# Spreading the decays of a chunked scan from three bfloat16 parts, with the early order of the program anew

## The chip, the cores and the metric

One core of one Trainium2 chip. The metric is the device time of one execution in microseconds (us); before, it is 664.39 us, the median of 3 runs (663.97 to 665.87).

## The reference

A chunked linear-attention scan, then a gated (GLU) layer, then a squared-ReLU layer:

```
la = log(clip(a, 1e-6, 1)); cum = cumsum(la)             # 4 batches, 8 heads, 768 steps
y[i] = sum_{j<=i} (C_i . B_j) exp(cum_i - cum_j) x_j  +  carried state, decayed
g, v = y @ w_gate, y @ w_val                             # 3072 x 256 @ 256 x 1536
z = (silu(g) * v) @ w_out                                # 1536 -> 256
out = relu(z @ w2_in)**2 @ w2_out                        # 256 -> 2048 -> 256
```

The inputs come as 32-bit floats, the weights as 64-bit floats, which the kernel converts. It splits operands into a high and a low fp32r part and sums three products (high x high, high x low, low x high), or runs some parts "exact" as plain fp32, which TensorE does in two passes.

## The kernel before

**The work.** The scan goes over 28 chunks of at most 112 steps (seven per batch). For a chunk, the decays `a` of its eight heads are spread over all 128 partitions, a scan on VectorE turns them into the decay matrix `L`, TensorE makes the scores `cb`, VectorE multiplies both into `mt`, and eight products `ys` give the outputs; the state goes through `st`, `turn` and back into `xa` for the next chunk. The GLU layer then runs in cells (a weight pair `j`, a range of chunks, exact or not): products `g` and `v`, a tanh on ScalarE, two multiplications on VectorE (`gate`, `times`), a split of the result on ScalarE and GpSimd (not for exact cells), and products into `acc`. The last layer runs over six tiles of 512 tokens.

**The early stage.** The first seven chunks (batch 0, `k < EARLY`) are handled differently from the 21 later ones. Their decays are spread by TensorE: `spread` (L548) multiplies a column of `pick`, broadcast, with the decays in `dv_all`, four heads to one PSUM tile `ab`, 56 fp32 products in all. Later chunks read the spread decays from DRAM (`decay`), where `keep_decays` (L333) stores them. `zeros` (L234) clears unused rows of `dv_all`, `load_a` (L244) loads, and `clip` (L252) bounds the values. Meanwhile the weight units are converted from 64-bit words: `share` and `mag` on ScalarE, `sign`, `clamp` and `shift` on VectorE (L380 to L406), then split into `hi` on ScalarE (`top`) and `lo` on GpSimd (`rest`, L412).

**The order.** Nothing is scheduled by the hardware: `Graph.order` (L50) simulates engines with a table of costs (the second argument of `g.add`), picks on each engine the ready operation with the lowest `prio`, and the program issues its instructions in that order. Each engine then runs its queue strictly in order, SP's queue of loads included. `PLAN` (L1027) holds priorities of chunks, weight units, splits and cells. Where the order leaves TensorE a gap of at least 110 ns before an operation that opens a PSUM tile, in the first 70 us of its own clock, `new` (L209) fills it with idle products of 256 columns:

```
if op.start - free >= 110:
    fills.append(int((op.start - free) / 110))
```

**The end.** `relu2` (L853) drains the last tile's two sums from PSUM in four half copies of 256 columns, two by ScalarE and two by VectorE, each with a store of its own (L909 to L933).

Of the kernel before, what the change touches and what calls it, by code (L numbers as in the profile page):

```python
# [8 lines left out]
F32 = mybir.dt.float32  # L9
# [25 lines left out]
class Graph:  # L35
# [14 lines left out]
    def order(self):  # L50
# [12 lines left out]
        while left:  # L63
            started = True
            while started:
                started = False
                for eng, ops in avail.items():
# [3 lines left out]
                    need = {}  # L71
                    for op in ops:
                        if best is not None and op.prio > best.prio:
                            continue
# [6 lines left out]
                        if all(len(free[p]) >= k for p, k in need.items()):  # L81
                            best = op
# [45 lines left out]
def kernel(  # L128
# [74 lines left out]
    dv = dv_all[0:R]  # L203
# [29 lines left out]

    def zeros():  # L234
# [4 lines left out]
        r = R  # L239
        while r < P:  # L240
            nc.vector.memset(dv_all[r : 2 * r], 0.0)
            r *= 2

    def load_a():  # L244
        v = a.rearrange("b h s -> (b h) s")
        nc.sync.dma_start(
            out=dv[:, :full, 1:], in_=v[:, : full * Q].rearrange("p (c q) -> p c q", c=full)
        )
        if full < NCB:
            nc.sync.dma_start(out=dv[:, full, 1 : 1 + S - full * Q], in_=v[:, full * Q :])  # L250

    def clip():  # L252

        for v in (dv[:, :full, 1:], dv[:, full:, 1 : 1 + S - full * Q]):
            nc.vector.tensor_scalar(v, v, 1e-6, 1.0, op0=ALU.max, op1=ALU.min)
# [39 lines left out]
    def setup_pick():  # L295
        nc.gpsimd.memset(pick, 0.0)
        nc.gpsimd.affine_select(
            out=pick, in_=pick, pattern=[[-1, H]], base=0,
            channel_multiplier=1, compare_op=ALU.not_equal, fill=1.0,
        )  # L300
# [14 lines left out]
    op_pick = g.add("POOL", 280, setup_pick, prio=-999)  # L315
# [12 lines left out]

    op_zero = g.add("DVE", 1000, zeros, prio=-960)
    ld_a = dma("SP", 2, 450, 200, load_a, [], -950)  # L330
    op_clip = g.add("DVE", 900, clip, [ld_a, op_zero], -950)

    def keep_decays(b):  # L333
        nc.sync.dma_start(
            out=decay[b].rearrange("c h q -> h c q"), in_=dv[b * H : (b + 1) * H]
# [3 lines left out]
        b: dma("SP", 1, 450, 400, lambda b=b: keep_decays(b), [op_clip], 300 + b)  # L339
# [84 lines left out]
    def chunk_ops(k, prio, after=(), load_after=()):  # L424
# [27 lines left out]
        if early:  # L452
# [9 lines left out]
            lb = dma("SP", 1, 480, 650, lambda: load_b(0, B), [op_eb[k % NEB], *load_after], ldp, [e])  # L462
            lc = dma("SP", 1, 480, 650, lambda: load_b(1, C), [op_eb[k % NEB], *load_after], ldp, [e])
# [622 lines left out]
```

## Time and profile before

| | before |
|---|---|
| median of 3 runs | 664.39 us |
| the profiled execution, its span | 664.27 us, 662.5 us |
| TensorE busy | 654.8 us, 99% of the span |
| VectorE, ScalarE, GpSimd busy | 63%, 50%, 34% |
| VectorE busy in the first 70 us | 58.1 us |
| TensorE's granted clock | 1.00 in every slice |

Times count from the start of the span. A row of the timeline gives start, length and the count of merged instructions; products are pipelined, their ends are modelled, and the end of one lies past the start of the next, so a rate is read from start to start. An idle product is named by the tile that it writes (`ab<-idle`).

### The profile page before, as it was taken

How to read it: one execution, taken by the hardware profiler on the slowest of the kernel's cores; microseconds unless marked ns; L12 is line 12 of the kernel's file. 1: busy time of each engine (PE TensorE's matmuls, PEld its weight loads, DVE VectorE, ACT ScalarE, POOL GpSimd, SP SyncE). 2: the span in 40 equal slices, each digit the busy share in tenths (PEclk: the TensorE clock that was granted, in tenths of full speed). 3: DMA queues.
4: the chain of work that ended last, by engine and by line, in shares of the span. 5: the costliest groups of instructions: out<-in, count | busy, mean ns of one | idle time of the engine just before them, and what ended most of it. 6: DMA issues, size and time to landing. Idle time of an engine off the chain costs nothing.

```text
span 662.5 us, 10931 instructions
## 1 busy us (share of the span) xinstructions
PE 654.8 (99%) x4297; PEld 560.9 (85%) x4297; DVE 415.5 (63%) x578; ACT 329.3 (50%) x634; POOL 221.9 (34%) x207
## 2 busy tenths in 40 slices
PE   9999999999999999999999999999999999999997
PEld 7888677899877777777788889999999999999996
DVE  7898796667565756677455698454455544544553
ACT  4667444455544444555544584444444444444443
POOL 4005864947555656656564541000000000000000
PEclk9999999999999999999999999999999999999999
DMA  7767447476465456752422220000000100000000
GB/s 176 210 129 153 134 84 145 88 134 123 100 126 94 81 108 113 171 129 50 142 64 63 64 65 0 1 33 1 1 33 0 33 1 1 33 1 0 33 1 33
DMA packets 134819, 48.88 MB, mean 74 GB/s; under 512 B 120304, under 2 KB 123376, under 8 KB 134768
## 3 DMA queue, kind: packets, MB, share of 16 engines
q1 hardware_dynamic: 134480, 47.92, 32.7%
q8 instruction: 34, 0.56, 0.4%
q10 hardware_dynamic: 288, 0.26, 0.1%
q14 instruction: 17, 0.14, 0.1%
HBM read 33.94 MB, written 3.22 MB: 56 GB/s over the span
## 4 chain that ended last, share of the span: by engine, by line
PE 97%; DMA 1%; SPq 0%; ACT 0%; issue 0%; DVE 0%; ACTq 0%
PE acc L892 21%; PE h L701 20%; PE g L701 18%; PE acc L819 16%; PE v L701 13%; PE ys L648 2%; PE ab L552 1%; PE cb L619 1%; DMA raw<-in_moe_w_val_dram 1%; PE ab L225 1%; PE cb L610 1%; PE turn L687 1%; PE g L225 1%; PE cb L225 0%; PE trb L225 0%
## 5 line engine op out<-in xcount | busy, mean ns | idle before, releaser
L892 PE MATMUL acc<-hi,p 128*128 128x256 f32 x768 | 152.1, 282 | 0.0
L892 PEld LDWEIGHTS acc<-hi,p 128*128 128x128 f32 x768 | 125.5, 191 | 3.9
L792 POOL TENSOR_TENSOR p<-t,p 128x512 fp32r<-128x512 f32 (+4 forms) x74 | 98.0, 1326 | 91.4 <-ACT p L787 89.3
L873 DVE TENSOR_TENSOR t<-t 128x512 f32<-128x512 f32 x96 | 69.2, 722 | 66.1 <-ACT t L870 66.0
L892 PE MATMUL acc<-lo,p 128*128 128x256 f32 x384 | 108.6, 283 | 0.0
L880 DVE TENSOR_TENSOR p<-t,p 128x512 fp32r<-128x512 f32 x96 | 67.8, 709 | 57.2 <-ACT p L876 57.2
L870 ACT ACTIVATE t<-h 128x512 f32<-128x512 f32 x96 | 57.5, 599 | 78.6 <-PE h L701 78.3
L768 DVE SCALAR_TENSOR_TENSOR t<-t,g 128x512 f32<-128x512 f32 (+6 forms) x92 | 51.9, 565 | 71.1 <-ACT t L765 71.0
L876 ACT ACTIVATE p<-t 128x512 fp32r<-128x512 f32 x96 | 60.5, 632 | 63.4 <-DVE t L873 59.9
L819 PE MATMUL acc<-p,hi 128*128 128x512 f32 (+4 forms) x296 | 85.7, 372 | 0.0
L892 PEld LDWEIGHTS acc<-lo,p 128*128 128x128 f32 x384 | 73.3, 191 | 3.5
L701 PE MATMUL h<-xh_all,hi 128*128 128x512 f32 x192 | 75.8, 395 | 0.0
L701 PE MATMUL h<-xl_all,hi 128*128 128x512 f32 x192 | 75.8, 395 | 0.0
L701 PE MATMUL h<-xh_all,lo 128*128 128x512 f32 x192 | 74.7, 389 | 0.0
L787 ACT ACTIVATE p<-t 128x512 fp32r<-128x512 f32 (+4 forms) x74 | 42.2, 571 | 62.5 <-DVE t L771 58.9
L765 ACT ACTIVATE t<-g 128x512 f32<-128x512 f32 (+6 forms) x92 | 46.1, 503 | 45.3 <-PE g L701 42.6
L701 PE MATMUL g<-xh_all,hi 128*128 128x512 f32 (+4 forms) x176 | 64.4, 366 | 0.0
L701 PE MATMUL g<-xh_all,lo 128*128 128x512 f32 (+4 forms) x176 | 61.4, 349 | 0.0
L701 PE MATMUL g<-xl_all,hi 128*128 128x512 f32 (+4 forms) x176 | 61.3, 349 | 0.0
L819 PEld LDWEIGHTS acc<-p,hi 128*128 128x128 f32 x296 | 52.1, 188 | 10.3 <-issue 2.9
L771 DVE SCALAR_TENSOR_TENSOR t<-t,v 128x512 f32<-128x512 f32 (+2 forms) x66 | 42.9, 649 | 21.6 <-PE v L701 17.2
L415 POOL TENSOR_TENSOR lo<-v,hi 128x1024 fp32r<-128x1024 f32 x17 | 42.8, 2535 | 32.2 <-ACT hi L410 32.0
(97 smaller groups left out, 1148.6 us busy)
## 6 DMA issues: line engine op xcount, KB each, us to landing
ab<-decay SPq DMA_DIRECT2D x21, 452.0 KB, 4.3
raw<-in_moe_w_out_dram SPq DMA_DIRECT2D x14, 512.0 KB, 5.1
raw<-in_moe_w_in_dram SPq DMA_DIRECT2D x8, 512.0 KB, 4.0
raw<-in_moe_w_gate_dram SPq DMA_DIRECT2D x6, 512.0 KB, 4.0
raw<-in_moe_w_val_dram SPq DMA_DIRECT2D x6, 512.0 KB, 5.1
xa<-in_x_dram SPq DMA_DIRECT2D x24, 112.0 KB, 4.1
out_dram<-o SPq DMA_DIRECT2D x10, 256.0 KB, 2.2
bc<-in_B_dram SPq DMA_DIRECT2D x18, 56.0 KB, 2.5
```

Of the source, the lines that this page charges most:

```text
L415: e.tensor_tensor(self.lo.t, self.v.t, self.hi.t.bitcast(F32), op=ALU.subtract)
L701: nc.tensor.matmul(ps, l, r, start=(i == 0), stop=(i == len(terms) - 1))
L765: nc.scalar.activation(t[:, :n], gg(), AF.Tanh, scale=0.5)
L768: nc.vector.scalar_tensor_tensor(tb.t[:, :n], tb.t[:, :n], 1.0, gg(), op0=ALU.add, op1=ALU.mult)
L771: nc.vector.scalar_tensor_tensor(tb.t[:, :n], tb.t[:, :n], 0.5, vv(), op0=ALU.mult, op1=ALU.mult)
L792: e.tensor_tensor(p[:, 1, :n], tb.t[:, :n], p[:, 0, :n].bitcast(F32), op=ALU.subtract)
L819: nc.tensor.matmul(ps, l, r, start=bank not in done_f, stop=f == NF - 1, skip_group_check=True,)
L870: nc.scalar.activation(new(tb, [P, TN], F32, "t"), ph.t, AF.Relu)
L873: nc.vector.tensor_tensor(tb.t, tb.t, tb.t, op=ALU.mult)
L876: nc.scalar.activation(new(pb, [P, 2, TN], F32R, "p")[:, 0, :], tb.t, AF.Copy)
L880: e.tensor_tensor(pb.t[:, 1, :], tb.t, pb.t[:, 0, :].bitcast(F32), op=ALU.subtract)
L892: nc.tensor.matmul(ps, pb.t[:, l, tk], r, start=(f == 0 and s == 0 and q % 2 == 0), stop=(f == NF2 - 1 and s == 2), skip_group_check=True,)
```

## The change

1. `dv` holds the decays three times (rows 0 to 31, 32 to 63, 64 to 95), and four steps, `part1`, `rest1`, `part2`, `rest2`, on ScalarE and VectorE in turn, make three bfloat16 parts of them in `dp`, whose sum is the fp32 value to about 24 bits. `spread` runs once over 96 rows in bfloat16, with ones of `pick` at each part's row. It is done in three lots: the first chunk, the next five, the last. The copies of later batches are stored from rows 64 to 95, which stay whole.
2. `Graph.order` puts an operation on VectorE or GpSimd that would need the port the other holds back, if that one will last more than 200 ns (`dodge`).
3. The low parts of two weight units are made on VectorE instead of GpSimd (`lo` in `PLAN`).
4. The last tile's sums leave in two copies of 512 columns, the first by VectorE, the second by ScalarE, with one store each.
5. Some costs of the table are set anew (the B, C and x transfers, the spread), and so are the priorities in `PLAN`.

```
+                    other = busy.get({"DVE": "POOL", "POOL": "DVE"}.get(eng))
                     for op in ops:
-                        if best is not None and op.prio > best.prio:
+                        at = op.prio
+                        if op.port and other and other.port and other.start + other.took > now + 200:
+                            at = (at[0] + PLAN["dodge"], at[1])
+                        if best is not None and at > best_at:
                             continue
...
-    pick = const.tile([P, H], F32, name="pick")
+    pick = const.tile([3 * R, H], BF16, name="pick")
-    dv_all = const.tile([P, NCB, Q + 1], F32, name="dv")
+    dp = const.tile([3 * R, NCB, Q + 1], BF16, name="dp")
...
+    dv_buf = Buf("ab")
+    dv = new(dv_buf, [P, NCB, Q + 1], F32, "dv")[0 : 3 * R]
...
+    def part1(c0, c1):
+        nc.scalar.activation(dp[:, c0:c1], dv[:, c0:c1], AF.Copy)
+    def rest1(c0, c1):
+        r = slice(0, 2 * R)
+        nc.vector.tensor_tensor(dv[r, c0:c1], dv[r, c0:c1], dp[r, c0:c1], op=ALU.subtract)
+    def part2(c0, c1):
+        nc.scalar.activation(dp[0 : 2 * R, c0:c1], dv[0 : 2 * R, c0:c1], AF.Copy)
+    def rest2(c0, c1):
+        r = slice(0, R)
+        nc.vector.tensor_tensor(dp[r, c0:c1], dv[r, c0:c1], dp[r, c0:c1], op=ALU.subtract)
...
+    for (c0, c1), at in zip(((0, 1), (1, full), (full, NCB)), PLAN["decay_at"]):
...
-        b: dma("SP", 1, 450, 400, lambda b=b: keep_decays(b), [op_clip], 300 + b)
+        b: dma("SP", 1, 450, 400, lambda b=b: keep_decays(b), op_clip, 300 + b, [dv_buf])
...
-                            v[:, j, :], pick[:, h : h + 1].to_broadcast([P, P]), dv_all[:, k, :],
+                            v[:, j, :], pick[:, h : h + 1].to_broadcast([3 * R, P]), dp[:, k, :],
...
-                o = g.add("PE", 1000, spread, [op_clip, op_pick, before.scans[-1] if before else None], prio, [ps, c.L], lat=250)
+                o = g.add("PE", 310, spread, [parts[k], op_pick, before.scans[-1] if before else None], prio, [ps, c.L], lat=250)
...
-            cuts = 2 if i == T // TN - 1 else 1
+            end = i == T // TN - 1
+            cuts = 1
...
-                    by_act = (m if cuts == 1 else c) == 0
+                    by_act = m == (1 if end else 0)
...
-        W1[u].split(abs(at) * 100, "POOL", [last_unit] if at < 0 else [])
+        W1[u].split(abs(at) * 100, "DVE" if PLAN["lo"][units.index(u)] else "POOL", [last_unit] if at < 0 else [])
...
-    chunk_at=[3.6, 14.8, 21.8, 0.0, 3.2, 18.0, 18.5],
+    chunk_at=[0, 18.4, 25.5, 1.0, 9.6, 12.8, 10.3],
...
+    dodge=3000,
+    lo=[0, 0, 0, 0, 0, 1, 1, 0, 0],
```

Over the whole program the order has 56 spread products before and after; idle products go from 119 to 179; fp32 products of 112 columns in the cells go from 48 to 24, fp32r products of 208 columns from 36 to 0, and those of 432 columns from 108 to 144.

VectorE's queue at the start, before: setup, the clips of `dv`, then scans of `ab` into `L` between the passes of the first weight units (`raw`, `v`).

```order
L241 MEMSET dv 32x791
L241 MEMSET dv 64x791
L255 TENSOR_SCALAR dv<-dv 32x6x112
L255 TENSOR_SCALAR dv<-dv 32x96
L561 SCALAR_TENSOR_TENSOR L<-ab,delta 128x452 x2
L395 SCALAR_TENSOR_TENSOR raw<-raw 128x1024
L400 TENSOR_SCALAR v<-v 128x1024
L404 SCALAR_TENSOR_TENSOR v<-v,raw 128x1024
L561 SCALAR_TENSOR_TENSOR L<-ab,delta 128x452 x2
L634 TENSOR_TENSOR mt_107<-cb,L 128x4x112 x2
```

The same place in the changed program (`dp` holds the parts; L599 is the scan, L672 the multiplication by the scores, L433 to L442 the weight unit):

```order
L264 TENSOR_SCALAR dv<-dv 96x112
L273 TENSOR_TENSOR dv<-dv,dp 64x113
L280 TENSOR_TENSOR dp<-dv,dp 32x113
L599 SCALAR_TENSOR_TENSOR L<-ab,delta 128x452 x2
L264 TENSOR_SCALAR dv<-dv 96x5x112
L672 TENSOR_TENSOR mt_107<-cb,L 128x4x112 x2
L433 SCALAR_TENSOR_TENSOR raw<-raw 128x1024
L438 TENSOR_SCALAR v<-v 128x1024
L709 TENSOR_TENSOR xl_all<-ys,xh_all 128x2x112
L442 SCALAR_TENSOR_TENSOR v<-v,raw 128x1024
L273 TENSOR_TENSOR dv<-dv,dp 64x565
```

The long memsets are gone, the first lot's subtractions stand before the first scan, and the second lot's clip and subtractions stand between the passes of the first weight unit, where the scan of the second chunk stood.

SP's queue of loads at the start, before (`eb` takes B and C of a chunk, `xa` its x, `raw` a weight unit):

```order
L246 DMA dv<-in_a_dram 32x6x112
L250 DMA dv<-in_a_dram 32x96
L374 DMA raw<-in_moe_w_out_dram 128x2x512 x2
L457 DMA eb_100<-in_B_dram 112x8x16
L457 DMA eb_100<-in_C_dram 112x8x16
L446 DMA xa_104<-in_x_dram 112x8x32
L374 DMA raw<-in_moe_w_gate_dram 128x2x512
L374 DMA raw<-in_moe_w_val_dram 128x2x512
L334 DMA decay<-dv 8x7x113 x3
```

and after:

```order
L253 DMA dv<-in_a_dram 96x1x112
L484 DMA xa_104<-in_x_dram 112x8x32
L495 DMA eb_100<-in_B_dram 112x8x16
L495 DMA eb_100<-in_C_dram 112x8x16
L412 DMA raw<-in_moe_w_gate_dram 128x2x512
L412 DMA raw<-in_moe_w_val_dram 128x2x512
L256 DMA dv<-in_a_dram 32x5x112 x3
L412 DMA raw<-in_moe_w_out_dram 128x2x512 x2
L253 DMA dv<-in_a_dram 96x1x96
```

The first chunk's x, B and C now stand ahead of all weights, a gate and value unit is loaded first, the loads of the second and third lot come behind it, and the stores of `decay` have moved further back, behind the loads of chunks 1 to 3.

TensorE's queue at the second chunk, before (L552 is the spread, L610 the scores):

```order
L468 MATMUL trb<-eye,eb_101 128x128 x2
L552 MATMUL ab<-dv,pick 128x113 x4
L648 MATMUL ys<-mt_107,xa_104 32x128 x8
L552 MATMUL ab<-dv,pick 128x113 x4
L610 MATMUL cb<-bct 128x112 x8
L687 MATMUL turn<-eye,st 16x128 x2
```

The same place in the changed program (L506 is the transposition, L739 the products `g` of an exact cell, L229 the filler):

```order
L506 MATMUL trb<-eye,eb_101 128x128 x2
L229 LDWEIGHTS idle
L229 MATMUL g<-idle 128x256
L739 MATMUL g<-xf,v 128x112 x8
L229 LDWEIGHTS idle
L229 MATMUL ab<-idle 128x256
...
L590 LDWEIGHTS pick
L590 MATMUL ab<-dp,pick 128x113
...
L648 MATMUL cb<-bct 128x112 x8
```

The output of the first chunk and its turn now stand ahead of this place, exact products of 112 columns have come in between, filler is spread around it, and each bfloat16 product has its weight load as an instruction of its own.

## Rows read from the trace of the kernel before

**Rows 1.** The chain that ended last, share of the span by engine.

```profile
PE 97%; DMA 1%; SPq 0%; ACT 0%; issue 0%; DVE 0%; ACTq 0%
```

**Rows 2.** TensorE's waits after the start: for what, us in total, times, longest.

```profile
PE turn L687 <- ACT st L682: 1.3, 1, 1.3
...
PE ys L648 <- issue: 1.1, 1, 1.1
```

**Rows 3.** Timeline of TensorE, first 75 us: start, us, line, operation, shape, count.

```profile
1.14 5.90 PE L225 MATMUL ab<-idle 128*128 128x256 bf16 x32 [1.14 <-DVE idle L207]
6.87 1.94 PE L552 MATMUL ab<-dv,pick 128*128 128x113 f32 x16
8.65 1.58 PE L225 MATMUL ab<-idle 128*128 128x256 bf16 x13
...
14.23 1.15 PE L610 MATMUL cb<-bct 64*128 64x112 f32 x16
...
17.93 0.64 PE L648 MATMUL ys<-mt,xa 128*32 128x128 f32 x16
...
28.89 0.94 PE L701 MATMUL g<-xf,v 128*128 128x224 f32 x4
...
64.46 0.65 PE L648 MATMUL ys<-mt,xa 112*32 112x128 f32 x16
```

**Rows 4.** The spread's group over the whole span: busy us, mean ns, idle before.

```profile
L552 PE MATMUL ab<-dv,pick 128*128 128x113 f32 x112 | 14.2, 276 | 0.0
```

**Rows 5.** Timeline of TensorE near 88 us, with bfloat16 scores of a late chunk.

```profile
88.12 0.57 PE L619 MATMUL cb<-bct 128*128 128x112 bf16 x8
88.50 0.44 PE L701 MATMUL v<-xh_all,hi 128*128 128x432 f32 x1
88.79 0.36 PE L701 MATMUL v<-xl_all,hi 128*128 128x432 f32 x1
88.98 0.36 PE L701 MATMUL v<-xh_all,lo 128*128 128x432 f32 x1
```

**Rows 6.** Timeline of TensorE near 105 us, products of 208 columns.

```profile
104.99 0.27 PE L701 MATMUL g<-xl_all,hi 128*128 128x208 f32 x1
105.10 0.27 PE L701 MATMUL g<-xh_all,lo 128*128 128x208 f32 x1
```

**Rows 7.** Timeline of VectorE, 13 to 64 us.

```profile
13.23 2.08 DVE L561 TENSOR_TENSOR_SCAN L<-ab,delta 128x452 f32<-128x452 f32 x2
15.41 1.16 DVE L634 TENSOR_TENSOR mt<-cb,L 128x448 f32<-128x448 f32 x2
16.48 1.22 DVE L395 SCALAR_TENSOR_TENSOR raw<-raw 128x1024 uint32<-128x1024 uint32 x1
17.61 0.68 DVE L400 TENSOR_SCALAR v<-v 128x1024 f32<-128x1024 f32 x1
18.33 1.22 DVE L404 SCALAR_TENSOR_TENSOR v<-v,raw 128x1024 uint32<-128x1024 uint32 x1
19.47 0.38 DVE L671 TENSOR_TENSOR xl_all<-ys,xh_all 128x224 fp32r<-128x224 f32 x1
...
34.11 0.39 DVE L771 SCALAR_TENSOR_TENSOR t<-t,g 128x224 f32<-128x224 f32 x1
...
60.40 3.31 DVE L404 SCALAR_TENSOR_TENSOR v<-v,raw 128x1024 uint32<-128x1024 uint32 x1
```

**Rows 8.** DMA issues by line: count, KB each, median us from issue to landing.

```profile
out_dram<-o SPq DMA_DIRECT2D x10, 256.0 KB, 2.2
...
out_dram<-o SPq DMA_DIRECT2D x2, 128.0 KB, 1.7
```

**Rows 9.** Timeline of ScalarE near 23 us, a weight conversion and what released it.

```profile
22.98 1.10 ACT L389 ACTIVATE raw<-raw 128x1024 int32<-128x1024 uint16 x1 [3.65 <-DMA raw<-in_moe_w_val_dram]
```

**Rows 10.** Line of the late scores: weight loads and products, ns min/median/max.

```profile
L619 PEld LDWEIGHTS <-bct x168: 95/98/102, 88.1 to 320.1; 128*128 128x128 bf16 x168
L619 PE MATMUL cb<-bct x168: 206/213/226, 88.1 to 320.1; 128*128 128x112 bf16 x144, 128*128 128x96 bf16 x24
```

More of the change, by code (lines that the diff above doesn't have):

```diff
@@ L237, in zeros, with load_a, clip @@
             nc.vector.memset(dv[:, full, 1 + S - full * Q :], 0.0)
[L239 to L244, printed above, removed]
-        v = a.rearrange("b h s -> (b h) s")
[L246 to L255, printed above, removed]
+    def load_a(c0, c1):
+        v = a.rearrange("b h s -> (b h) s")
+        t0, n = c0 * Q, min(Q, S - c0 * Q)
+        if c1 - c0 == 1:
+            src = v[:, t0 : t0 + n]
+            src = bass.AP(src.tensor, src.offset, [[0, 3], [S, R], [1, n]])
+            nc.sync.dma_start(out=dv[:, c0, 1 : 1 + n], in_=src)
+        else:
+            for i in range(3):
+                nc.sync.dma_start(
+                    out=dv[i * R : (i + 1) * R, c0:c1, 1 : 1 + n],
+                    in_=v[:, t0 : t0 + (c1 - c0) * n].rearrange("p (c q) -> p c q", c=c1 - c0),
+                )
+    def clip(c0, c1):
+        v = dv[:, c0:c1, 1 : 1 + min(Q, S - c0 * Q)]
+        nc.vector.tensor_scalar(v, v, 1e-6, 1.0, op0=ALU.max, op1=ALU.min)
+    def part1(c0, c1):
[8 more added lines that the diff above has]
+        nc.vector.tensor_tensor(dp[r, c0:c1], dv[r, c0:c1], dp[r, c0:c1], op=ALU.subtract)
     def setup_dve():
@@ L296, in setup_pick @@
         nc.gpsimd.memset(pick, 0.0)
[L297 to L300, printed above, removed]
+        for i in range(3):
+            nc.gpsimd.affine_select(
+                out=pick, in_=pick, pattern=[[-1, H]], base=-i * R,
+                channel_multiplier=1, compare_op=ALU.not_equal, fill=1.0,
+            )
     def setup_bc():
@@ L925, in store @@
                     def store(ob=ob, by_act=by_act, r0=t0 + m * 256 + c * (w // 2)):
-                        q = nc.scalar if by_act and cuts == 2 else nc.sync
+                        q = nc.scalar if by_act and end else nc.sync
                         q.dma_start(
@@ L932, in relu2 @@
                     o = g.add("ACT" if by_act else "DVE", 690 // cuts, drain, [bk], prio - GATE, [ab[m], ob])
-                    dma("ACT" if by_act and cuts == 2 else "SP", 1, 480, 700, store, [o], prio, [ob])
+                    dma("ACT" if by_act and end else "SP", 1, 480, 700, store, [o], prio, [ob])
         return o1, bk
@@ L1027 @@
 PLAN = dict(
-    chunk_at=[3.6, 14.8, 21.8, 0.0, 3.2, 18.0, 18.5],
-    unit_at=[4.1, 0, 22.6, 19.4, 20.4, 41.5, 34.2, 27.1, 30.0],
-    split_at=[-0.1, -21.6, 22.5, -12.5, -9.6, 27.7, -0.1, -18.9, -33.9],
+    chunk_at=[0, 18.4, 25.5, 1.0, 9.6, 12.8, 10.3],
+    unit_at=[0.6, 14.2, 26.4, 24.5, 25.5, 36.5, 42.9, 26.0, 29.8],
+    split_at=[-1.7, -37.7, 65.8, -3.7, 4.5, -30.7, -27.2, 49.0, 13.5],
     cells=[
+        (2, 3, 7, 0),
+        (4, 0, 3, 0),
+        (3, 3, 7, 0),
         (5, 3, 7, 0),
-        (4, 0, 3, 0),
+        (1, 3, 7, 1),
+        (3, 0, 3, 0),
+        (4, 3, 7, 0),
+        (0, 3, 7, 1),
+        (1, 0, 3, 0),
+        (0, 1, 3, 1),
         (5, 0, 3, 1),
-        (3, 3, 7, 1),
         (2, 0, 2, 1),
-        (0, 3, 7, 1),
-        (4, 3, 7, 0),
-        (0, 1, 2, 1),
-        (2, 5, 7, 0),
-        (1, 3, 7, 0),
-        (2, 2, 3, 1),
-        (0, 0, 1, 1),
-        (0, 2, 3, 1),
-        (3, 0, 3, 0),
-        (1, 0, 3, 0),
-        (2, 3, 5, 1),
-    ],
-    pace=[-5, 2.65, 13],
-    second=[34, 5, 6],
+        (0, 0, 1, 1),
+        (2, 2, 3, 1),
+    ],
+    pace=[-5, 2.67, 9],
+    second=[20, 6, 1],
     gate=[30000, 30000],
     lead=2.5,
+    decay_at=[-950, 381, 1562],
     spare=0,
     warm=70000,
+    dodge=3000,
+    lo=[0, 0, 0, 0, 0, 1, 1, 0, 0],
 )
```

30 lines of the change are left out of this document (20 added, 10 removed).

## The prediction

> **What bounds the kernel.** I read the chain of waits first: 97% of the chain that ends last is TensorE's own work [rows 1]. TensorE's list of waits then has only two after the start, 1.1 us before an output `ys` and 1.3 us before a `turn`, 2.4 us in all [rows 2]. TensorE is thus never short of work, but in the first 68 us part of that work is filler: 119 idle products, which the order puts where its table expects TensorE to wait [rows 3]. So two things set the time: how long TensorE's real products take, and how much filler and waiting the first stage still needs. What VectorE, ScalarE or GpSimd save later costs or gains nothing, unless it makes TensorE wait.
>
> All sums are made against the profiled execution, 664.27 us, which is 0.12 us under the median of the runs (664.39). What lies around the span stays as it is.
>
> **1. The spread.** Before, 56 fp32 products spread the decays, and each shows as two passes: 112 passes, a group of 14.2 us [rows 4]. The rows of the timeline run a little past the start of what follows; from start to start the first 16 passes take 8.65 - 6.87 = 1.78 us [rows 3], 0.111 each, which makes 12.5 us for seven chunks. Between 12.5 and 14.2 I take 13.0. After, there are 56 bfloat16 products of 113 columns over 96 rows. The nearest row is the bfloat16 scores, eight of 112 columns in 88.50 - 88.12 = 0.38 us, 0.0475 each [rows 5]; so 2.7 us. If one bfloat16 product took as long as one fp32 pass (0.111) it would be 6.2. I take the nearer row: **minus 10.3 us** (minus 6.8 at the other end). Each new product has a weight load of its own, and so have those eight.
>
> The Trainium skill, in "TensorE: Matmul & The Clock Gate", section "Back-to-back issue gap", puts a stream of weight load and product pairs with 128 columns at some 81 ns a pair. By it the spread would be 4.5 us and the sum 1.8 us higher, an estimate. The eight scores of this trace ran at 47.5 ns, so the row decides.
>
> **2. The order of cells anew.** Counted over both programs, 24 fp32 products of 112 columns go (48 passes at 0.111: 5.3 us), 36 products of 208 columns go (105.10 - 104.99 = 0.11 each: 4.0 us [rows 6]), and 36 of 432 columns come (88.98 - 88.79 = 0.19 to 0.2 each [rows 5]: 7.0 us). **Minus 2.3 us**. It falls due on TensorE, so all of it counts.
>
> **3. The filler.** 119 idle products become 179. Thirteen have a row of 1.58 us, less the 0.16 it runs over: 1.42, 0.109 each [rows 3]. The first 32 took 5.7 us, 0.18 each, and I take that for the first 32 of after too. Sixty more at 0.109: **plus 6.5 us**. They cannot be skipped once they stand in the queue: this part of the gain is given back for certain.
>
> **4. Waits beyond the filler.** The two of before (2.4 us) go with their places; what comes is the open cost. Without any wait the sum is 664.27 - 10.3 - 2.3 + 6.5 - 2.4 = 655.8 us, the floor. For the new waits I follow the two busiest engines to the output `ys` of the last early chunk.
> - TensorE: 1.1 us to begin, 173 fillers (5.7 + 141 x 0.109 = 21.1), the spread 2.7, seven scores at 1.08, six earlier outputs at 0.57, eleven fp32 sets of 224 columns at 0.77, 24 passes of 112 columns at 0.111 [rows 3] (each row less the 0.07 to 0.17 by which it runs past the next start), and 13 pairs of turns at two such passes, 2.9: together 49.8 us.
> - VectorE: its first scan needs 42 fillers, a transposition and four spreads, so it starts near 8.7 us. From there to the last scores' multiplication stand 14 scans at 1.04, 14 multiplications at 0.535, five weight units at 1.13 + 0.72 + 1.14, five `xl_all` at 0.38 less 0.08, five pairs of gate products (three at 2 x 0.39, two shorter) 3.4 [rows 7], and of the decays two clips and four subtractions. For the latter the nearest row is again the `xl_all` subtraction, 0.38 us for 224 elements, and the weight unit's pass, 1.2 us for 1024: between them 565 elements cost about 0.75 and 113 about 0.28, with the clips 2.7 us. Together 44.7, so 53.4 us if VectorE never idles.
>
> VectorE arrives 3.6 us after TensorE. So TensorE waits **plus 3.6 us** in this stage; afterwards its products of 432 columns last longer than what VectorE does for them, and it sets the pace again. The ends: nothing, if VectorE's passes overlap better than start to start; 5 us, if it idles a little between.
>
> **5. What I cost at nothing.** The six ScalarE copies (about 2.5 us by the same lengths) and the first lot's five steps lie under the first 42 fillers, which end near 8.0 us; without that cover the first scan would be later by what they exceed. The port rule moves work, it adds none: it can spare VectorE a collision like the 3.31 us that one 1.2 us pass took while GpSimd made low parts [rows 7], and that one came where TensorE did not wait. The memsets that go (two long ones of the unused rows) lay before VectorE's first scan, where it waits anyway. On SP's queue the x load of the first chunk now passes B and C, and both weight loads of the unit stand behind them: no weight transfer is ahead of B and C any more, so the transposition is not later than its filler. The decay stores now wait for the third clip, and behind them stand weight and B/C loads of chunk 3, covered by 31 fillers (3.4 us) around its transposition. Two low parts move from GpSimd to VectorE late, behind products of 336 columns; TensorE has other cells in its queue there, and the list of waits had none there [rows 2]. At the end two half copies on each engine become one of 512: the last copy starts sooner, since nothing precedes it on its bank, but a store of 256 KB lands in 2.2 us, of 128 KB in 1.7 [rows 8]. I take zero, with 0.5 either way.
>
> **Sum:** 655.8 + 3.6 = **659.4 us**, minus 0.7%.
>
> **The rivals.**
> - **Loads come late.** The two waits of before both began on ScalarE, which stood behind a weight load: 3.65 us in the first [rows 9], while outputs and turns were queued behind it. The changed order still has weight conversions ahead of turns on ScalarE. One such wait that VectorE cannot absorb adds 3.65: 663.0 us; half of it, 661.2. For: SP issues more small loads ahead of the first weights. Against: the filler is longer, so there is more cover. Chance 0.17, a third of it still under 662.3.
> - **The filler covers everything.** If VectorE's stage packs as the table of costs assumes, the waits vanish: 655.8 us. Against it stands the sum of VectorE's rows. Chance 0.08.
> - **The weight loads set the pace of the spread.** One of bfloat16 takes 98 ns [rows 10]; if 56 of them do not overlap they make 5.5 us, 2.8 more than taken: 662.2. Against: the same loads stood before the eight quick scores. Chance 0.06.
> - **Slower: the second lot of decays stops VectorE.** Its clip, two copies and two subtractions stand in the queues of VectorE and ScalarE among the first weight units, and its load is issued behind a unit's 1 MB. Both queues keep their order, so a late load stops all early chunks at once. Three waits of the size in rows 9 make 11 us: 670.4. It decides from 6.9 us of idle VectorE (659.4 to 666.3), after which the change is slower. For: it is a new five-step chain between two full engines. Against: the spread that needs the second lot stands some ten microseconds after the first. Chance 0.07.
>
> That a bfloat16 product would still run as two passes I leave without a chance: the late scores are 21 chunks of eight products, and the trace has 168 of them, one pass each [rows 10].
>
> **How the numbers follow.** My forecast has 0.62: 657.8 to 660.8 for waits of 2 to 5 us. A measurement of this kernel tells about 0.3%, 2 us, from no change, so faster means under 662.4. Faster: 0.62 + 0.08 + 0.06 + a third of the late loads, 0.06, makes 0.82. Same: the rest of them, 0.11. Slower: 0.07. The range goes from the floor, 655.8, to 663.0, the late-load case; only the slower case and what lies past one late load stay outside.
>
> **What would show it.** In the profile after: the spread's group at 56 products and about 3 us from start to start; 179 idle products; TensorE's list of waits with 2 to 5 us in the first 60 us, most of it released by VectorE's multiplications `mt` or by what follows from them; the last early output near 53 to 55 us, where it was at 64.5 [rows 3]; no wait later. Wrong would be: waits over 6 us, a wait behind a load, or any in the stage of 512 columns.

## The result, and the profile after

The changed kernel takes **671.25 us** (median of 4 runs, 670.61 to 672.26) against 664.18 (663.55 to 665.87) for the kernel before on the same chip: ratio 1.0113, 95% interval 1.0098 to 1.0127. It is slower by 1.1%, where 0.7% faster was forecast. The profiled execution took 671.73 us, with a span of 669.8.

On the page, the chain that ended last, by engine, which answers to [rows 1]:

```profile
PE 83%; DMA 6%; DVE 5%; ACT 2%; issue 1%; SPq 1%; POOL 1%; DVEq 0%; POOLq 0%; ACTq 0%
```

TensorE made 97% of it before. TensorE's waits (for what, us in total, times, longest us), which answer to [rows 2]:

```profile
PE acc L857 <- DVE t L809: 2.2, 2, 1.2
PE g L739 <- ACT xf L701: 1.7, 1, 1.7
PE trb L229 <- DVE dv L242: 1.1, 1, 1.1
PE ys L686 <- POOL mt L632: 1.1, 1, 1.1
PE g L739 <- DVE lo L453: 1.0, 1, 1.0
PE trb L506 <- DMA eb<-in_B_dram: 0.7, 1, 0.7
```

TensorE's timeline, which answers to [rows 3]:

```profile
7.24 0.38 PE L506 MATMUL trb<-eye,eb 128*128 128x128 f32 x2
7.46 0.56 PE L590 MATMUL ab<-dp,pick 96*128 96x113 bf16 x8
7.86 1.58 PE L229 MATMUL cb<-idle 128*128 128x256 bf16 x13
...
55.22 0.64 PE L686 MATMUL ys<-mt,xa 112*32 112x128 f32 x16
...
60.22 1.72 PE L739 MATMUL g<-xf,v 128*128 128x432 f32 x4 [1.74 <-ACT xf L701]
```

The eight new spread products run from 7.46 to 7.86, 0.05 us each from start to start, and the last early output stands at 55.2 where it was at 64.46 [rows 3]. So the last early output comes 9.2 us sooner, and the program takes 7 us longer. The page's group of the spread, which answers to [rows 4], has 56 products; each overlaps the next, so its busy time is above 56 x 0.05 = 2.8:

```profile
L590 PE MATMUL ab<-dp,pick 96*128 96x113 bf16 x56 | 4.1, 213 | 0.0
```

The wait of 1.74 us at 60.22 is explained on ScalarE. Its timeline there, which answers to [rows 9]:

```profile
58.61 1.10 ACT L427 ACTIVATE raw<-raw 128x1024 int32<-128x1024 uint16 x1 [3.67 <-DMA raw<-in_moe_w_val_dram]
59.61 0.34 ACT L803 ACTIVATE t<-g 128x224 f32<-128x224 f32 x1
59.85 0.32 ACT L701 ACTIVATE xf<-ys 128x192 f32<-128x192 f32 x1
```

ScalarE stood 3.67 us before a weight conversion, because the load had not landed; the copy `xf` of the last early output was queued behind it, and TensorE waited for `xf`.

To see where the time went I use four starts on TensorE's timeline, in us: the last early output, the first product of 512 columns, the first `h` of the last layer, and the last product. They are read from the profiled execution of each kernel that the text needs; `e1` to `e17` and `b1` are the experiments of the next section. The execution of e7 was 1.9 us above the median of its runs, those of the others in the table within 0.8:

| kernel | early output | first 512 | first `h` | last product |
|---|---|---|---|---|
| before | 64.5 | 169.1 | 385.1 | 658.2 |
| changed | 55.2 | 171.2 | 390.9 | 665.5 |
| e1: changed, 32 bytes of padding | 55.9 | 170.7 | 387.0 | 660.2 |
| e7: e1, spread four times | 62.0 | 174.2 | 390.5 | 663.8 |
| e10: e1, longer conversions | 55.6 | 176.8 | 393.1 | 666.4 |
| e12: e1, shorter conversions | 56.5 | 168.3 | 384.7 | 657.9 |
| b1: before, bfloat16 spread | 65.3 | 170.0 | 386.5 | 659.7 |
| e11: before, longer conversions | 65.1 | 169.8 | 385.8 | 658.9 |
| e13: before, shorter conversions | 61.1 | 165.6 | 381.6 | 654.8 |
| e14: new order, half the filler | 53.3 | 164.0 | 378.4 | 653.0 |
| e16: new order, whole filler | 56.1 | 166.8 | 381.2 | 655.8 |

Between the early output and the first product of 512 columns the kernel before needs 104.6 us, the changed one 116.0: the 9.2 us are given back there, and 2 more. The windows of TensorE from the early output to that product, before and e1 (start and end, length, busy time and count, then the other engines), show of what this consists:

```profile
64.46:169.08 104.62, 104.57 (x740) 87.97 (x740) 76.14 (x110) 51.84 (x122) 71.21 (x64) 1.00 0.60 118
```

```profile
55.92:170.66 114.74, 109.93 (x760) 91.94 (x760) 81.52 (x117) 58.65 (x129) 68.94 (x62) 1.00 0.59 114
```

Of the 10.1 us more in e1, 4.8 are idle time and 5.4 are work. The new order puts work of the cells behind the early output that stood ahead of it, so an earlier output is not the same as a gain. Then, in the changed kernel, the stage from there up to `h` takes 219.7 us instead of 216.0, and the last layer 274.6 instead of 273.1, though neither has a wait and the clock is 1.00. These are two separate losses.

### The profile page after: what moved, and what is told of

Same layout as the page of the kernel before. It is cut to its first block, busy times and chain, and to the rows that moved or that the text cites. A ratio compares the mean times of both kernels' runs of the same rounds, so it can differ in the third digit from the quotient of the medians.

```text
span 669.8 us, 10829 instructions
## 1 busy us (share of the span) xinstructions
PE 656.1 (98%) x4253; PEld 552.5 (82%) x4253; DVE 412.6 (62%) x576; ACT 332.8 (50%) x635; POOL 214.9 (32%) x207
## 4 chain that ended last, share of the span: by engine, by line
PE 83%; DMA 6%; DVE 5%; ACT 2%; issue 1%; SPq 1%; POOL 1%; DVEq 0%; POOLq 0%; ACTq 0%
PE acc L930 21%; PE h L739 20%; PE g L739 14%; PE acc L857 13%; PE v L739 12%; DMA raw<-in_moe_w_val_dram 2%; PE ys L686 2%; PE cb L657 1%; DVE L L620 1%; DVE v L442 1%; DMA raw<-in_moe_w_out_dram 1%; DMA eb<-in_C_dram 1%; DMA ab<-decay 1%; DMA dv<-in_a_dram 1%; DVE raw L433 1%
## 5 line engine op out<-in xcount | busy, mean ns | idle before, releaser
L830 POOL TENSOR_TENSOR p<-t,p 128x512 fp32r<-128x512 f32 (+3 forms) x74 | 102.9, 1392 | 99.2 <-ACT p L825 99.0
L911 DVE TENSOR_TENSOR t<-t 128x512 f32<-128x512 f32 x96 | 67.1, 698 | 70.8 <-ACT t L908 70.8
L857 PE MATMUL acc<-p,hi 128*128 128x512 f32 (+3 forms) x296 | 87.4, 377 | 0.5 <-POOL p L830 0.5
L806 DVE SCALAR_TENSOR_TENSOR t<-t,g 128x512 f32<-128x512 f32 (+5 forms) x88 | 51.2, 582 | 55.3 <-ACT t L803 50.3
L739 PE MATMUL h<-xl_all,hi 128*128 128x512 f32 x192 | 76.3, 397 | 0.0
L739 PE MATMUL h<-xh_all,hi 128*128 128x512 f32 x192 | 76.2, 397 | 0.0
L739 PE MATMUL h<-xh_all,lo 128*128 128x512 f32 x192 | 75.5, 393 | 0.0
L803 ACT ACTIVATE t<-g 128x512 f32<-128x512 f32 (+5 forms) x88 | 45.6, 518 | 58.5 <-PE g L739 57.4
L825 ACT ACTIVATE p<-t 128x512 fp32r<-128x512 f32 (+3 forms) x74 | 42.5, 575 | 62.6 <-DVE t L809 62.0
L739 PE MATMUL g<-xh_all,hi 128*128 128x512 f32 (+3 forms) x172 | 63.5, 369 | 0.0
L739 PE MATMUL g<-xh_all,lo 128*128 128x512 f32 (+3 forms) x172 | 61.0, 355 | 1.0 <-DVE lo L453 1.0
L739 PE MATMUL g<-xl_all,hi 128*128 128x512 f32 (+3 forms) x172 | 60.8, 353 | 0.0
L857 PE MATMUL acc<-p,lo 128*128 128x512 f32 (+3 forms) x148 | 54.0, 365 | 0.0
```

Source lines behind the costliest of these rows:

```text
L739: nc.tensor.matmul(ps, l, r, start=(i == 0), stop=(i == len(terms) - 1))
L803: nc.scalar.activation(t[:, :n], gg(), AF.Tanh, scale=0.5)
L806: nc.vector.scalar_tensor_tensor(tb.t[:, :n], tb.t[:, :n], 1.0, gg(), op0=ALU.add, op1=ALU.mult)
L825: nc.scalar.activation(p[:, 0, :n], tb.t[:, :n], AF.Copy)
L830: e.tensor_tensor(p[:, 1, :n], tb.t[:, :n], p[:, 0, :n].bitcast(F32), op=ALU.subtract)
L857: nc.tensor.matmul(ps, l, r, start=bank not in done_f, stop=f == NF - 1, skip_group_check=True,)
```

## The experiments

Each time is a median in us. Behind it stand, in brackets, its ratio to runs of the kernel before on the same chip, whose median was 663.5 to 663.9 us throughout, and the 95% interval of that ratio.

### The place of the tiles in memory

The timeline of TensorE in the stage of 512 columns, before, and then the same after:

```profile
302.83 0.39 PE L701 MATMUL g<-xl_all,hi 128*128 128x512 f32 x1
...
305.80 0.39 PE L701 MATMUL g<-xh_all,lo 128*128 128x512 f32 x1
```

```profile
300.47 0.40 PE L739 MATMUL v<-xl_all,hi 128*128 128x512 f32 x1
...
305.61 0.40 PE L739 MATMUL g<-xh_all,lo 128*128 128x512 f32 x1
```

From the first row to the second lie 13 products before, 2.97 us, 0.2285 each; after, 22 products and 5.14 us, 0.2336. The same instruction on the same shape takes 2% longer. What differs is where tiles lie: the change takes `dv` (3,164 bytes a partition) out of the constant tiles and puts `dp` (1,582) there, so all that follows, weight tiles included, stands 1,568 bytes lower, while the split inputs `xh_all` and `xl_all`, which stand ahead, stay.

**e1** pads the changed kernel by 32 bytes, so that the weight tiles stand at 128 modulo 512 bytes, as do the inputs, and as they do before. **e2**, **e3** and **e6** pad the kernel before by 32, 64 and 128.

```
     dp = const.tile([3 * R, NCB, Q + 1], BF16, name="dp")
+    const.tile([P, 8], F32, name="pad")
```

> The changed kernel with 32 unused bytes per partition behind the decays, so that the weight, split and scratch tiles start at a multiple of 64 bytes again, as in the kernel before; nothing else differs. Theory A (place in memory): in the changed kernel these tiles lie 32 bytes off a multiple of 64, and that is why 512-column products take 0.2327 us from start to start in the GLU stage instead of 0.2285 and 0.2336 instead of 0.2311 in the last stage. 864 x 0.0042 + 576 x 0.0025 = 5.1 us: the time falls from 671.3 to about 666.2, the rates go back to 0.2285 and 0.231, and the waits between 60 and 160 us stay. Rival B (order): the products are slower because other engines work at other moments; then rate and time stay, 670 to 672. Rival C: the memory also slows VectorE and GpSimd; then the waits between 60 and 160 us shrink too and the time falls under 664.

> The kernel before with 32 unused bytes per partition behind its decays, so that all later tiles move 32 bytes off a multiple of 64. Theory A: 512-column products slow down to 0.2327 and 0.2336 us as in the changed kernel, and the time rises by about 5 us to 669.3. Rival B: no change, 664.2.

> The kernel before with 64 unused bytes instead, so that all later tiles move but stay at multiples of 64. Theory A: no change, 664.2 within 1 us, rates 0.2285 and 0.231. If moving the tiles at all is what matters, the time changes as with 32 bytes.

> The kernel before with 128 unused bytes, after 32 and 64 bytes both slowed it. Theory: the weight tiles must start at a multiple of 128 bytes, which they do in the kernel before and here; then rates (0.2285 and 0.231) and time (663.9) do not change, within 1.2 us. Rival: what counts is where they lie against the tokens' tiles, which have stayed, or a multiple of 256; then it slows as with 32 and 64, to 667 or 668.

Measured: e1 666.44 (1.0039, 1.0025 to 1.0053), e2 666.82 (1.0047, 1.0032 to 1.0063), e3 667.93 (1.0069, 1.0046 to 1.0093), e6 666.27 (1.0042, 1.0027 to 1.0057). An unused tile of 32 bytes is worth 4.8 us in the changed kernel, and costs the kernel before 2.9. TensorE's timeline in e1:

```profile
299.76 0.40 PE L740 MATMUL g<-xh_all,hi 128*128 128x512 f32 x1
...
303.63 0.39 PE L740 MATMUL g<-xh_all,lo 128*128 128x512 f32 x1
```

17 products in 3.87 us, 0.2276: the old rate is back. That 64 and 128 bytes also cost time refutes a plain alignment of the weights to either.

**e8** puts 64 bytes ahead of everything, **e9** 64 ahead and 448 more behind the decays, **e15** 256 behind the decays:

```
+    const.tile([P, 16], F32, name="pad")
     xh_all = const.tile([P, 2, T], F32R, name="xh_all")
...
     dv_all = const.tile([P, NCB, Q + 1], F32, name="dv")
+    const.tile([P, 112], F32, name="pad2")
```

> The kernel before with 64 bytes ahead of everything that it keeps: the split inputs and the weight tiles all stand 64 bytes further, so their places against each other are those of before (both at 192 modulo 512 bytes, where before has both at 128). If the places against each other count: no change, 663.9 us within 1.5, and a 512-column product from start to start 0.2285 us in the GLU part. If the weights' own place counts (in two runs a move of the weight tiles alone by 64 or 32 bytes gave 0.2333): 667 to 668 us and 0.2333 us again.

> The kernel before with 64 bytes ahead of the split inputs and 448 behind the decays: the weight tiles stand 512 bytes further (128 modulo 512, as before) and only the inputs, masks and states move by 64 bytes. If the places against each other count: 667 to 668 us and 0.233 us from start to start of a 512-column product in the GLU part; if only the weight tiles' own place modulo 512 counts: no change, 663.9 us within 1.5 and 0.2285.

> The kernel before with 256 bytes behind the decays: the weight tiles stand at 384 modulo 512 bytes, the split inputs at 128 as before. If a difference of 0 modulo 256 is enough: no change, 663.9 within 1.5, and 0.2285 us from start to start in the GLU part. If it must be 0 modulo 512: 667 to 668 us and 0.231 to 0.233.

Measured: e8 663.81 (1.0006, 0.9990 to 1.0021), e9 666.94 (1.0040, 1.0025 to 1.0055), e15 663.87 (1.0003, 0.9993 to 1.0014). So it is the place of the one group against the other that counts, not the place itself, and a difference of 0 modulo 256 bytes is enough. e2, e3, e6 and e9 and the changed kernel, with other differences, are slow; before, e1, e8 and e15 are not. Why the difference matters stays open: the products into `acc`, which read neither split input, are slower in e9 as well (0.231 against 0.228 us on average, without the longer gaps between groups).

### Does TensorE's own work set the early stage?

**b1** is the kernel before, with its order, and only the spread in bfloat16 (its parts made in two lots, tiles at the same place modulo 512). **e4** is e1 with half the filler, **e7** is e1 with each spread product issued four times.

```
-                fills.append(int((op.start - free) / 110))
+                fills.append(int((op.start - free) / 220))
```

```
+                        for _ in range(4):
                             nc.tensor.matmul(
                                 v[:, j, :], pick[:, h : h + 1].to_broadcast([3 * R, P]), dp[:, k, :],
```

> The kernel before with the bfloat16 spread alone: its own order and table of costs stay; the parts are made in two lots directly after the clips (five more passes on VectorE and ScalarE, the second lot's last subtraction behind the first scan), three copies of the decays are loaded, and all later tiles lie at the same place modulo 512 bytes as before. TensorE saves 10.3 us of products up to 52 us. VectorE is delayed by 0.7 to 2 us at the start and idled some 6 us between 8 and 64 us before. If TensorE bound the old order's early stage, 5 to 8 us are saved: 656 to 659. If VectorE and the loads bind it, 0 to 3: 661 to 664. If the new chain holds up the first scans, it is slower: 665.

> The changed kernel with the 32 bytes and with half of the idle products (one per 220 ns of expected gap instead of one per 110). If filler is paid in full, as the prediction's sum had it, some 90 fewer at 0.109 us save up to 9 us against the same kernel with all of them. If VectorE bounds the early stage, as the prediction's step on waits had it, TensorE only waits instead, and the time stays within 1.5 us. If TensorE's clock falls for want of work, the time rises and the granted clock in the first slices shows under 1.00.

> The changed kernel with the 32 bytes, with each bfloat16 spread product issued four times into the same place: TensorE then works on the spread for 56 x 4 x 0.049 = 11 us, 8.2 more, near the 13 of the kernel before. If TensorE's time in the early stage counted in full (the prediction's steps 1 and 3), the time rises by 8.2 to 674.6. If VectorE bounds that stage (step 4: TensorE waits 3.6 us and has its filler besides), only what exceeds the wait counts: plus 3 to 5, 669.5 to 671.5. If more is hidden, the early gain of the bfloat16 spread was small: under plus 2.

Measured: b1 665.88 (1.0023, 1.0008 to 1.0037), e4 665.87 (1.0032, 1.0022 to 1.0042), e7 668.27 (1.0070, 1.0053 to 1.0087). b1 has 10 us less on TensorE, and its last early output comes at 65.3, no earlier than before: TensorE now waits, 2.7 us for the x of a chunk and 2.1 for `st`, the longest of its list of waits. Its first 55 us (length, PE busy, PEld, DVE, ACT, POOL, clock, DMA share, GB/s):

```profile
0.00:55.00 55.00, 48.59 (x477) 40.89 (x478) 46.18 (x75) 32.96 (x83) 13.69 (x37) 0.94 0.77 179
```

It idles 6.4 us there, where the kernel before idles 2.2 (its row stands further down), and the granted clock is 0.94 instead of 1.00, which is worth at most 3.3 us. So part of what the shorter products save went into a lower clock, and b1 also adds the steps that make the parts: it shows what the spread is worth in that order, not what TensorE's time alone is worth.

e4 has 95 idle products fewer, as the rows of the idle tile's weight loads show, in the changed kernel and in e4:

```profile
L229 PEld LDWEIGHTS <-idle x179: 95/98/154, 1.1 to 58.1; 128*128 128x128 bf16 x179
```

```profile
L230 PEld LDWEIGHTS <-idle x84: 95/98/153, 1.1 to 58.0; 128*128 128x128 bf16 x84
```

At 0.109 us each that is 10.4 us of TensorE, and the time falls by 0.6, less than the runs of either kernel differ among themselves (about 2 us). The first 55 us of e4:

```profile
0.00:55.00 55.00, 45.46 (x438) 34.54 (x439) 45.61 (x76) 34.16 (x88) 14.32 (x38) 0.97 0.85 185
```

TensorE idles 9.5 us there instead of 4.1 in e1, and the clock is 0.97, which costs at most 1.7 us. e7 puts 8.2 us on TensorE; the early output moves by 6.1, the time by 1.8. TensorE's work in the early stage, taken away or added, reaches the end of the program only in small part.

### The chain of weight loads

From the chain that ended last, in order of time, the weight loads between 40 and 100 us (start us, us, what), before and then after:

```profile
48.30 7.83 DMA raw<-in_moe_w_val_dram
```

```profile
52.67 5.85 DMA raw<-in_moe_w_val_dram
...
64.03 5.88 DMA raw<-in_moe_w_val_dram
...
75.74 4.99 DMA raw<-in_moe_w_val_dram
```

The last three units are loaded one after the other into two raw buffers; a load starts when an earlier unit is converted. In the new order they start at 52.7, 64.0 and 75.7 us; before at 48.3, 64.2 and 75.9. Nine microseconds less of early chunks do not bring them forward. **e10** and **e11** issue ScalarE's second conversion of these units three times, in e1 and in the kernel before; **e12** and **e13** leave two of their passes out. **e5** makes the two low parts of e1 on GpSimd again.

```
-            nc.scalar.activation(self.v.t, self.words(raw)[1].bitcast(F32), AF.Abs, scale=65536.0)
+            for _ in range(self.times):
+                nc.scalar.activation(self.v.t, self.words(raw)[1].bitcast(F32), AF.Abs, scale=65536.0)
...
+        W1[kind, j] = Unit(srcs, at * 100, times=3 if kind == "gv" and j > 2 else 1)
```

```
         def share(self, raw):
+            if self.cut:
+                return
...
         def sign(self, raw):
+            if self.cut:
+                return
```

> The changed kernel with 32 bytes of padding, and ScalarE's second conversion of each of the last three gate and value units issued three times instead of once (the same result each time): six more ScalarE instructions of 1.15 us between 58 and 85 us, 2.3 us per unit and 6.9 in all, on the way from a weight load to the next. If the weights' chain of load, conversion and free buffer sets when the stage of narrow products runs: 3 to 7 us slower than the 666.4 of the kernel without them. If TensorE and the early chunks set it: under 1.5 slower.

> The same six extra conversions in the kernel before, whose TensorE waited for no weight in that stretch: if its early chunks left the weights a lead of some us, under half of what the same work costs the changed kernel, 0 to 3 us over 663.9; if the weights' chain sets the time there as well, as much as in the changed kernel, 3 to 7 us.

> The changed kernel with 32 bytes of padding, in whose last three gate and value units the first conversion on ScalarE and the sign pass on VectorE are left out (their weights lose sign and lowest bits, so this part is not computed). Each of the three is 1.15 us of ScalarE and 1.2 us of VectorE shorter, and the raw buffer is free after ScalarE's remaining pass. If the chain of weight loads and conversions sets when the stage of narrow products runs: 3 to 6 us faster than the 666.4 with them, 660.5 to 663.5, about what the forecast wanted. If TensorE, the early chunks or the other waits set it: under 1.5 faster.

> The same left out in the kernel before. If its early chunks and TensorE's own work set the time there, it gains under 1.5 us over its 663.9; if weights' chain sets it as well, 3 or more.

> The changed kernel with the 32 bytes, with the two low parts that had moved to VectorE made on GpSimd at the same places of the order. In the run with the 32 bytes alone, TensorE waited 1.0 us at 112 us for such a low part, and up to 1.1 us near 109 us for gate products of VectorE. Theory: the move causes these two; then 1 to 2 us are saved against that run (666.4 to about 665). Rival: on GpSimd each takes 2.4 us instead of 1.2, so the wait grows by about 1 us for each: 667 to 668.

Measured: e10 672.52 (1.0125, 1.0104 to 1.0146), e11 664.77 (1.0012, 1.0002 to 1.0022), e12 663.96 (1.0000, 0.9990 to 1.0010), e13 660.92 (0.9954, 0.9939 to 0.9970), e5 667.62 (1.0066, 1.0051 to 1.0081). The same six passes, 6.9 us, cost the changed kernel 6.1 us and the kernel before 0.9: there the conversions have a lead, here none. Leaving passes out gave 2.5 us, between the two cases that were expected (3 to 6, or under 1.5), and e13 missed both of its cases: the kernel before gains as much, 2.8. The table of starts tells the two apart. In e12 the early output stays, and the time from it to the first product of 512 columns falls from 114.8 to 111.8 us. In e13 that time is 104.5, as before, and the early output comes 3.4 us earlier than before. ScalarE's timeline shows why, the kernel before first and then e13:

```profile
56.20 1.12 ACT L389 ACTIVATE raw<-raw 128x1024 int32<-128x1024 uint16 x1 [3.11 <-DMA raw<-in_moe_w_val_dram]
...
57.84 0.20 ACT L682 ACTIVATE st<-ys 128x32 f32<-128x32 f32 x1
```

```profile
54.10 0.19 ACT L688 ACTIVATE st<-ys 128x32 f32<-128x32 f32 x1
```

Before, ScalarE stands 3.11 us in front of the first of these conversions, and the state's copy `st`, which TensorE's `turn` waits for [rows 2], is queued behind it; with that conversion gone, `st` runs 3.7 us earlier. So the kernel before has one hold by these loads, ahead of its last early output, and a lead after it. In the changed kernel the holds come after that output, one unit after the other.

The windows show how much (stretch, its length, PE busy, PEld, DVE, ACT, POOL, clock, DMA share, GB/s), before, e1, e10 and e12:

```profile
0.00:55.00 55.00, 52.76 (x534) 46.92 (x535) 45.96 (x74) 31.10 (x79) 12.46 (x35) 1.00 0.76 179
55.00:100.00 45.00, 43.55 (x249) 33.25 (x248) 36.97 (x47) 26.21 (x49) 30.59 (x18) 1.00 0.48 107
100.00:170.00 70.00, 69.95 (x559) 62.57 (x558) 46.21 (x75) 34.25 (x90) 45.53 (x48) 1.00 0.66 122
```

```profile
0.00:55.00 55.00, 50.95 (x527) 41.56 (x528) 45.43 (x75) 34.40 (x87) 13.84 (x38) 1.00 0.83 181
55.00:100.00 45.00, 42.58 (x225) 31.80 (x223) 35.34 (x44) 24.90 (x44) 28.82 (x19) 1.00 0.40 100
100.00:170.00 70.00, 67.61 (x537) 60.12 (x536) 47.10 (x75) 33.46 (x87) 40.09 (x46) 1.00 0.72 127
```

```profile
55.00:100.00 45.00, 39.64 (x181) 27.95 (x180) 30.25 (x39) 29.53 (x43) 25.04 (x15) 0.96 0.30 87
```

```profile
55.00:100.00 45.00, 44.65 (x239) 33.73 (x238) 32.50 (x46) 23.54 (x44) 28.22 (x21) 1.00 0.44 110
100.00:170.00 70.00, 67.92 (x542) 60.70 (x542) 46.12 (x74) 33.36 (x87) 39.35 (x45) 1.00 0.66 121
```

From 55 to 100 us, TensorE idles 2.4 us in e1, 5.4 in e10 (where the granted clock falls to 0.96 as well, which is at most 1.8 us of the 6.1), 0.35 in e12. From 100 to 170 us it idles 2.4 in e1 and 2.1 in e12, 0.05 before: this part is not the chain's; TensorE's list of waits in e1 names `g` behind `lo`, 1.0 us, and three of half a microsecond there, `acc` behind VectorE's `t`, `acc` behind GpSimd's `p` and a transposing load of `cb`. So the chain of loads is worth some 2.5 us, and does not explain all that e1 lost. e5 shows that the low parts on VectorE are no cause: on GpSimd the wait for `lo` is 2.2 us instead of 1.0, and the time 1.2 longer.

### An order that expects slower loads

**e14** is e4 with slower loads in the table that sets the order, and priorities to suit. **e16** is the same with the whole filler. **e17** is another order for the same loads, with the whole filler.

```
-                ... dma("SP", 1, 450, 1650, lambda s=s, src=src: self.load(raw, s, src), after, prio, [raw])
+                ... dma("SP", 1, 450, 2300, lambda s=s, src=src: self.load(raw, s, src), after, prio, [raw])
-        o = g.add("DMA", move, None, [i], prio, bufs, lat=1700)
+        o = g.add("DMA", move, None, [i], prio, bufs, lat=2200)
...
-    chunk_at=[0, 18.4, 25.5, 1.0, 9.6, 12.8, 10.3],
-    unit_at=[0.6, 14.2, 26.4, 24.5, 25.5, 36.5, 42.9, 26.0, 29.8],
+    chunk_at=[9.7, 9.9, 18.6, 0.1, 0.1, 14.9, 1.2],
+    unit_at=[1.4, 4.2, 42.2, 21.1, 37.0, 158.8, 75.5, 37.6, 43.2],
...
-    lo=[0, 0, 0, 0, 0, 1, 1, 0, 0],
+    lo=[1, 0, 0, 1, 0, 0, 1, 1, 1],
```

> A candidate: the changed kernel with 32 bytes of padding and half its filler, its order laid out anew for slower loads: in the table a weight load moves data for 2300 ns instead of 1650 and every load lands 2200 ns after instead of 1700 (the traces show 4.5 to 5.5 us from issue to landing of a weight load), with priorities to suit, five low parts on VectorE. If late weights are what the changed kernel loses, an order that expects them gives 659 to 663 us; if what counts lies elsewhere, or the new order has new waits, 664 or more.

> The candidate of the slow-load order with the whole filler, an idle product for 110 ns of an expected gap instead of 220. If the wait near 10 us and the lower clock behind it (0.66 granted between 10 and 20 us) held up the early stage: the clock reads 1.00 there and the time is 1 to 3 us under 659.75, 656.8 to 658.8. If loads and VectorE set the early stage whatever TensorE's clock, within 1 of 659.75. If the filler is paid in full (some 90 more idle products at 0.109 us): 664 and more.

> Another order found for the same slower loads of the table, with other priorities, also with the whole filler. If it is the costs of the loads that matter, it too comes below the kernel before: 657 to 662 us. If the first candidate was one lucky order: 664 or more.

Measured: **e14 659.75** (0.9940, 0.9921 to 0.9960), e16 661.85 (0.9972, 0.9959 to 0.9985), e17 663.38 (1.0000, 0.9991 to 1.0010). e14 is faster than both kernels. All three are faster than e1 with its 666.44, and TensorE idles 1.4 us from 55 to 170 us in e14 and 1.7 in the other two, where it idles 4.8 in e1. They differ from e1 in cells and low parts as well, e14 also in its filler, so the loads' part in that is not shown by itself. e16 missed, and TensorE's timeline shows how, e14 first and then e16:

```profile
7.36 3.00 PE L230 MATMUL trb<-idle 128*128 128x256 bf16 x26
13.11 0.80 PE L507 MATMUL trb<-eye,eb 128*128 128x128 f32 x2 [2.75 <-DMA eb<-in_B_dram]
13.71 2.76 PE L230 MATMUL cb<-idle 128*128 128x256 bf16 x12
16.40 2.05 PE L649 MATMUL cb<-bct 64*128 64x112 f32 x16
```

```profile
11.18 5.84 PE L230 MATMUL trb<-idle 128*128 128x256 bf16 x52
16.86 0.38 PE L507 MATMUL trb<-eye,eb 128*128 128x128 f32 x2
...
19.79 1.15 PE L649 MATMUL cb<-bct 64*128 64x112 f32 x16
```

The B that the transposition needs is there at 13.1 us. Half the filler ends before that, so TensorE waits 2.75 us, and the clock falls behind the wait (sixteen passes of scores take 2.05 us instead of 1.15). The window of 10 to 20 us in e14 has a granted clock of 0.66:

```profile
10.00:20.00 10.00, 7.25 (x48) 5.07 (x49) 9.05 (x13) 5.81 (x15) 2.31 (x1) 0.66 0.98 176
```

The whole filler keeps the clock at 1.00 but ends at 16.9, 3.7 us after the 13.1 at which B was there in e14; the last early output comes 2.8 us later, the first 512-column product too. Here idle products are paid for; in e1 they nearly were not, for with half of them away TensorE waited instead (e4). e17 lies between its two forecasts and no better than the kernel before, so slower loads in the table are not enough by themselves: e14 is one good order, not proof of a rule.

## Why the prediction was wrong, point by point

The forecast was 659.4 us; 11.9 are missing. e1 splits them: 4.8 for the place of the tiles, 7.0 for the rest.

- **What was left out.** The prediction priced instructions, queues and waits, and took every product that stays at its old length: a term put at nothing without a reason. Removing `dv_all` from the constant tiles moved the weight tiles, and every product of 512 columns became 2% longer. No step had this, neither did a rival. It is 4.8 us by e1, and 2.9 the other way round by e2.
- **Step 1, the spread.** The duration was right: 0.05 us each and 2.8 in all, where 2.7 stood. The 81 ns a pair of the Trainium skill's "TensorE: Matmul & The Clock Gate", section "Back-to-back issue gap", do not hold for these products. Wrong was to count the saving as time: with the old order it brought none (b1, in part by a lower clock), and 8.2 us put back cost 1.8 (e7).
- **Step 2, the cells.** No experiment tested it by itself. Summed on TensorE's timeline from start to start up to the first product of 512 columns, the cells' products take 2.0 us less in e1 than before, where 2.3 stood.
- **Step 3, the filler**, "given back for certain". Wrong: half of it away gave 0.6 us, not some 10 (e4). It was paid where it lasted longer than the wait it covers, as in e16.
- **Step 4, the waits.** For the early stage the step was near: 53 to 55 us were named for the last output, 55.2 came. In e1 TensorE idles 4.1 us in the first 55, 2.9 without the start, where 3.6 stood, though behind loads of B and VectorE's `t`, not behind `mt` as was said. The sentence that failed is the next one, that TensorE afterwards "sets the pace again": from 55 to 170 us it idles 4.8 us in e1, where nothing stood, and 1.5 before. In the kernel before the weights had a lead (e11). Idle time of TensorE in the first 170 us is 3.7 us before and 8.9 in e1 (length less PE's busy time in the three windows of each), where the forecast had 4.7 with the start. That is 4.2 of the 7.0. Shorter conversions give 2.5 of the 7.0 back (e12), all of it between 55 and 170 us; the idle time of 100 to 170 us, 2.3 us more than before, hardly changes with them.
- **The other 2.8 us** are TensorE's own time, by the same sums from start to start as in step 2: the spread went from 13.1 to 3.2 us, 9.9 less where 10.3 stood; the filler from 15.1 to 22.5, 7.4 more where 6.5 stood; the cells give 0.3 less than forecast; and transpositions, turns and outputs, which the sum left as they were, take 1.3 more from start to start, which may be waits too short for the list.
- **Step 5.** The low parts on VectorE were rightly nothing or a small gain (e5). From the last product's start to the end of the span it is 4.3 us in both kernels, so the tail is nothing, as said. The port rule was not tried alone.
- **The rivals.** "Loads come late" is the one that happened, by its own mechanism: ScalarE behind a weight load, 3.67 us, with TensorE's copy behind it. It was priced as one wait on top of the forecast, 663.0; it was a chain of three loads, worth some 2.5 us (e12), and with the place of the tiles right the kernel came to 666.4 by other losses besides. "The second lot of decays stops VectorE", the slower rival, gave 670.4, near the result, but for another reason: TensorE waits at most 1.2 us at a time in the first 55 us. Among the signs named for a wrong forecast, "a wait behind a load" is there, and TensorE's list of waits after adds up to 9.3 us, where over 6 was named.

## What to carry to other kernels

Where the bound is handed from one engine to another, a saving is worth what the next chain leaves of it: follow the loads of the stage after it to their issue and ask whether they start any earlier; the test is to lengthen that chain in both kernels, as e10 and e11 do, and to read the start of the next stage, not busy time. When a change alters the size of any kept tile, compare the places of the tiles behind it with those ahead, and the rate of an untouched product from start to start, before arguing about anything else. Filler was nearly free where what it covers came no sooner (e4: 0.6 us for 10.4 of it), and cost 2.1 us of the program where it ran 3.7 us past that moment (e16 against e14), though it also kept the clock at 1.00.

## What the runs showed of the hardware

- A product of 512 columns with fp32r operands takes 0.2276 to 0.2285 us from start to start when weight tiles and split inputs stand at a difference of 0 or 256 modulo 512 bytes, and up to 0.2336 when the difference is 32, 64, 128, 448 or 480 modulo 512 bytes (whole program: 0.4 to 0.7%). Moving everything together changes nothing (e8).
- After a wait of 2.75 us in e14 the granted clock was 0.66 between 10 and 20 us, a mix of the levels 1.2 and 2.4 GHz; sixteen passes of scores took 2.05 us in it, 1.15 at 2.4 GHz. In b1 it was 0.68 between 20 and 30 us, around a wait of 2.74 us.
